# Eight products or seven for Q block 4 and FFN block 12 of the first two chunks, and a head played from words, in a linear attention and FFN kernel

## The chip, the core and the metric

One core of a Trainium2 chip runs the kernel. Its engines are TensorE (PE in the profile; its weight loads are listed as PEld), VectorE (DVE), ScalarE (ACT), GpSimd (POOL) and SyncE (SP, which here only issues DMAs; ACT and POOL can issue them too). Each engine has a queue of its own and takes its instructions in order; semaphores hold an instruction back until what it reads is there. The metric is the time of one execution in microseconds (us), as the median of the runs; the aim is a lower one.

## The reference

`x` has 2048 tokens of D = 640 values. It is normalised over the 640 values, and two branches read the result:

```
xn  = layernorm(x)
q, k, v = xn @ wqkv, cut in three, then into 32 heads of 20
phi(t) = where(t > 0, t + 1, exp(t)) + 1e-6
kv  = sum over tokens of phi(k) (outer) v          # per head
z   = sum over tokens of phi(k)                    # per head
o   = (phi(q) @ kv) / (phi(q) . z + 1e-6)
s   = o @ wo
g   = silu( relu(xn @ w1) @ w2 )                   # w1: 640 x 1728, w2: 1728 x 640
out = x + s * g
```

All tensors are bfloat16.

## The kernel before

**Tiles and stages.** The tokens are 16 tiles of 128, or 4 chunks of 512. Data with the features on the partitions (`xnT`) has 5 blocks of 128 features. FFN columns are 13 blocks of 128 (0 to 12) and a half block of 64; Q columns are 5 blocks (0 to 4). A product block `H j f` (FFN block f of chunk j) or `Q j f` is five matmuls of 128 x 128 by 512 columns, one for each block of features. K is made tile by tile, as five matmuls for each of two halves of 320 columns.

The stages follow each other. The *head* normalises tiles 0 to 7, makes K for them and the first FFN blocks. Then come Q, the rest of K, and the FFN blocks; the product `G` of xn and phi(k) with the denominators; the small products that fold v and wo into one matrix (`kv`, `W`); and last the two output products, `u` for the gate and `o` for the attention, tile pair by tile pair.

**Seven products for eight.** Where two halves of columns meet two halves of the 512 leading features and two chunks, `unit` (line 1169) makes the 2 x 2 block product with seven products and sums of operands (Strassen's scheme in Winograd's form), where eight would be needed. Products 1, 2, 3, 4, 5, 6 and 7 are steps `s1` to `s7`. The fifth block of 128 features is added to products 2, 3 and 4 and, as product 8, to step 7, so that a unit has 2+3+3+3+2+2+2+1 = 18 matmuls. The operand sums are made on VectorE: `h_S`, `q_S`, `m_S` and `k_S` on the weights, `h_T` (`T0` for chunks 0 and 1, `T1` for chunks 2 and 3) on `xnT`. In a unit VectorE also adds pairs of products in PSUM and ScalarE copies two of them. Units are called `a`, `b` (FFN blocks i and i + 6, chunks 0, 1 and chunks 2, 3), `p`, `q` (Q blocks f and f + 2), `k` (K of two tiles), `m` (Q block 4 with FFN block 12), `g`, `u` and `o`. Before the change `m` exists for chunks 2 and 3 alone (`m1`); for chunks 0 and 1 the four blocks are made directly, as `Q04`, `Q14`, `H112`, and FFN block 12 of chunk 0 in the head.

**The head.** K of tiles 0 to 3 and the FFN blocks 4, 5, 10, 11 and 12 of chunk 0 (`HP`) start before the normalisation is known: x is centred (`centre`), transposed on TensorE (`transposes`) and copied out of PSUM (`xcT_copy`), and the factor 1/sigma comes later, for K by the scale of the evacuation, for the FFN blocks by a product with `rsyB` on VectorE (`scale_h`, word `ZS`). Means come from half statistics on VectorE (`bn`) and from an accumulating copy on ScalarE (`mean_act`); variances of all tiles from two `bn_stats` and a `bn_aggr` on VectorE (`bn`, `aggr`; both with the norms in `LN_stats`), and the root from GpSimd. Tiles 4 to 7 are normalised (`LN_norm`) and transposed by a DMA that SP issues (`xnT_dma`, line 702). The order of the head is that of the calls in the source: the loads at the top, then a list of calls for tiles 0 to 3, then five head blocks and four K tiles with the lists `after` of what VectorE is given behind each.

**What sets the order.** Every instruction is recorded with what it reads and writes. From `PROGRAM` (line 343), a list of words, `play` (line 1569) records the work after the head: a word is a step of a unit (`a0.s5`), a block (`H111`), or a piece of work for another engine (`SQ`: the sums `q_S`; `xa`: a load; `n8`: norm of tile 8; `y7`: adding tile 7 of phi(k) to a sum over tokens, by a DMA of GpSimd). `place` (line 189) then puts the records in the order of each engine's queue. TensorE and SP keep the recorded order. The other engines keep it up to `end_of_head`; behind that, the planner takes, by its own costs and due times, one of the next 60 that can run.

**Queues that the change touches.** SP issues, in this order: x tile 0, the K weights in four parts (features 0, 1, 2, and 3 with 4), w1 column groups 2 and 5, x tiles 4 and 5, w1 group 6, x tiles 6 and 7, w1 groups 0 and 3, then the transposes of tiles 4 to 7, x tiles 8 and 9, `wq` (the weights of Q), the transposes of tiles 0 to 3, x tiles 10 and 11, and so on. ScalarE issues x tiles 1, 2 and 3. Column group d of w1 holds FFN blocks 2d and 2d + 1.

Of the kernel before, what the change touches and what calls it, by code (L numbers as in the profile page):

```python
# [4 lines left out]
ALU = mybir.AluOpType  # L5
# [340 lines left out]
H110 H112 H14 H111 T0 H15 SQ SK xa Q14 a0.s1 a0.s5 Q04 a0.s6 p1.s5 p1.s1 n8 wa xb a0.s2 a0.s7 p1.s6 rb a0.s3 a0.s4 p1.s3 a1.s5 a1.s1 wb p1.s7 p1.s2 a1.s6 xc n9 SH1 p1.s4 a1.s2 Kb8 a1.s7 n12 n11 p0.s1 n10 n13 a1.s3 p0.s5 Ka8 p0.s6 n14 a1.s4 n15 y7 p0.s2 a2.s5 a2.s1 p0.s7 Ka12 a2.s6 Kb12 p0.s3 a2.s2 p0.s4 y8 a2.s3 a2.s7 hh0 hh1 T1 a2.s4 b0.s1 b0.s5 Ka11 b0.s6 k1.s1 k1.s5 b0.s2 k1.s6 b0.s7 b0.s3 k1.s7 k1.s2 b0.s4 k1.s3 k1.s4 Kb15 q0.s1 q0.s5 b1.s1 q0.s6 b1.s5 q0.s2 b1.s6 q0.s7 y6 q0.s3 b1.s3 q0.s4 mv6 b1.s7 b1.s2 y2 k2.s5 k2.s1 b1.s4 a3.s5 y3 k2.s6 Kb11 y9 a3.s1 k2.s2 k2.s7 k2.s3 a3.s6 k2.s4 a3.s2 a3.s7 a3.s3 q1.s1 q1.s5 a3.s4 q1.s6 b2.s5 q1.s2 SM y12 b2.s1 y13 Ka15 y0 q1.s7 w2a b2.s6 y4 y1 y14 GT1 GT2 y5 y15 q1.s3 y11 q1.s4 b2.s7 zm b2.s3 GS0 GT3 b2.s2 b3.s1 b2.s4 b3.s5 SH2 y10 b3.s6 m1.s5 m1.s1 b3.s2 b3.s7 m1.s6 b3.s3 m1.s2 b3.s4 m1.s7 zs b4.s5 GT4 m1.s3 b4.s1 m1.s4 c1 b4.s6 b5.s5 b5.s1 w2d c0 b4.s7 b4.s2 b4.s3 b5.s6 b4.s4 g0.s5 w2b g0.s1 b5.s7 b5.s3 b5.s2 zc g0.s6 b5.s4 dn g0.s3 g1.s1 GS1 g1.s5 g1.s6 g0.s7 g0.s2 w2c g1.s7 g1.s3 wv0 ZS uT3 wo do0 g1.s2 g1.s4 g0.s4 wv1 sl rc0 uSa0 uSb0 uT2 uT1 do3 do1 u0.s1 u0.s5 kv1 u0.s6 rc1 kv0 W5 u0.s7 u0.s2 W4 uT4 uSa2 dv1 u0.s3 W2 u0.s4 W1 W3 W0 xre dv0 uSa1 u1.s1 oT uSb2 uSb1 u1.s5 u2.s1 u2.s5 u1.s6 u2.s6 u2.s2 uSa4 u2.s7 oS0 u1.s7 u1.s3 u2.s3 u1.s2 u2.s4 u1.s4 do2 o0.s5 o0.s1 u4.s5 o0.s6 u4.s1 o0.s2 o0.s3 uSb4 o0.s7 u4.s6 o0.s4 u4.s2 o1.s1 oS2 uSa6 u4.s7 oS1 o1.s5 o1.s2 o1.s6 uSa3 u4.s3 o1.s3 o1.s7 u4.s4 o1.s4 u3.s5 o2.s1 u3.s1 rc3 o2.s5 o2.s2 o2.s6 u3.s6 uSb3 o2.s7 dv3 o2.s3 uSa5 u3.s7 o2.s4 u3.s2 o3.s1 rc2 u3.s3 u3.s4 oS3 uSb6 dv2 o3.s2 o3.s5 oS4 o3.s6 u5.s1 u5.s5 o3.s7 o3.s3 uSb5 u5.s6 u5.s2 o3.s4 u5.s7 u5.s3 o4.s1 u5.s4 o4.s5 o4.s2 o4.s6 u6.s1 u6.s5 oS5 u6.s6 o4.s3 o4.s7 u6.s7 o4.s4 u6.s3 oS6 o6.s1 o6.s5 u6.s2 o6.s6 u6.s4 o6.s2 o6.s7 o6.s3 e3 uSa7 o6.s4 u7.s1 o5.s5 o5.s1 u7.s5 o5.s6 u7.s6 o5.s7 o5.s2 o5.s3 u7.s2 o5.s4 e0 f0 uSb7 u7.s7 u7.s3 f3 e1 u7.s4 f1 l0 l1  # L346
# [3 lines left out]
def bass_recurrent_scan__linear_attn_block__dense_activation_relu__prompt_kernel(  # L350
# [292 lines left out]

    def LN_stats(t):
        bn(t, 0)
        bn(t, 1)
        aggr(t)
# [3 lines left out]
    def LN_norm(t):  # L653
        norms.append(sc.op("DVE", lambda eng: eng.tensor_scalar(
            out=xn[:, t, :], in0=xin[:, xs(t), :], scalar1=mv[:, t, 0:1], scalar2=rsy[:, t:t + 1],
            op0=ALU.subtract, op1=ALU.mult), R=[("xin", xs(t)), ("mv", t), ("rsy", t)], W=[("xn", t)]))
        xnT_dma(t)
# [174 lines left out]

    bn(0, 0)
    mean_act(0, HN)
    half_mean_dve(0)
    centre(0)
    mean_act(1, 0)
    transposes(0, 0)  # L840
    xcT_copy(0, 0, 0, "DVE")
    centre(1)
    fill(3)
    K_mm(0, 2, 0, 1)
    transposes(1, 6)
    xcT_copy(0, 0, 1, "DVE")
    mean_act(2, 0)
    xcT_copy(1, 6, 0, "DVE")
    xcT_copy(1, 6, 1, "ACT")
    K_mm(0, 2, 1, KA)  # L850
    K_mm(1, 4, 0, KA)
    centre(2)
# [36 lines left out]
    K_relu(3, 0)
# [397 lines left out]
    def m_unit(jp):  # L1287
        w1l = w1_p[NW - 1]

        def out(half, j, b):  # L1290
            if half:
                sc.op("ACT", lambda eng: eng.activation(out=hT[:, NF - 1, schunk(j)], in_=ps[b], func=ACTF.Relu),
                      R=[("ps", b)], W=[("hT", j, NF - 1)])
# [71 lines left out]
    HP = (4, 5, 10, 11, 12)  # L1365

    def K_tile(t, b):
        K_mm(t, b)
        K_exp(t, b)
        K_relu(t, b)  # L1370
# [157 lines left out]
    def w2_last():  # L1528
# [4 lines left out]
    single = {  # L1533
        "rb": scale_rows,
# [114 lines left out]
    LC = [0, 160, 320]  # L1649
# [252 lines left out]
    def silu_table():  # L1902
# [16 lines left out]
        "oS": o_S,  # L1919
        "st": lambda t: s_tile(t, two_banks()),  # L1920
        "l": s_last,
# [6 lines left out]
        "y": z_add,  # L1928
    }
# [31 lines left out]
```

## Time and profile before

| | us |
|---|---|
| median of the runs | 202.73 |
| lowest, highest of three runs | 202.44, 232.07 |
| span of the profiled execution | 201.4 |
| TensorE busy, share of the span | 197.8, 98% |
| VectorE busy, share of the span | 175.1, 87% |
| ScalarE busy, share of the span | 130.9, 65% |
| GpSimd busy, share of the span | 37.9, 19% |
| DMA: read from HBM, written to it | 15.81 MB, 5.24 MB |

Times come from one profiled execution, with a span of 201.4 us from its first to its last instruction; the runs' median of 202.73 us is 1.3 us more. The granted clock of TensorE is full throughout. "Busy" counts an instruction from its start to its end, and matmuls overlap, so that their pace is read from the distance of their starts, and not from their lengths. Rows of a timeline give start, length, engine, line, operation, output and inputs, count, and in brackets how long the engine had been idle and what ended it. The chain of waits is followed back from the last instruction, at each step to what released it. Names that begin with `reg` are large buffers that hold one thing after another, and buffer numbers are left out; `psT` is PSUM.

### The profile page before, as it was taken

What the parts mean: (1) busy time and instruction counts of PE and PEld (TensorE: products, weight loads), DVE (VectorE), ACT (ScalarE), POOL (GpSimd) and SP (SyncE); (2) the same over time, 40 slices, a digit from 0 to 9 for tenths busy, and PEclk for the clock granted to TensorE, in tenths of its full rate; (3) what the DMA queues carried; (4) which work ended last, traced back from release to release, by engine and by line L of the source; (5) the groups of instructions that cost most, each with busy time, mean ns of one, the idle gap of its engine ahead of it and who ended that gap; (6) DMA issues with size and microseconds to landing.
All of it is one profiled execution on the core that took longest, in us unless ns stands there. A gap on an engine that the chain in (4) does not pass through costs nothing.

```text
span 201.4 us, 3693 instructions
## 1 busy us (share of the span) xinstructions
PE 197.8 (98%) x1340; PEld 122.6 (61%) x1340; DVE 175.1 (87%) x413; ACT 130.9 (65%) x273; POOL 37.9 (19%) x66
## 2 busy tenths in 40 slices
PE   8999999999999999999999999999999999999995
PEld 7655644455455454445654777777777777767773
DVE  5988999999999888999975999999779786985674
ACT  6598957998999999978653224371555555445643
POOL 3174060363134654152200000000000000000000
PEclk9999999999999999999999999999999999999999
DMA  6977974765545896575910987865961244012103
GB/s 196 326 211 120 264 174 30 189 164 119 116 92 107 163 260 131 102 142 104 245 34 2 324 217 207 263 201 145 373 232 65 68 163 165 0 67 68 65 33 98
DMA packets 38471, 30.43 MB, mean 151 GB/s; under 512 B 13749, under 2 KB 38453, under 8 KB 38453
## 3 DMA queue, kind: packets, MB, share of 16 engines
q1 hardware_dynamic: 32581, 23.28, 41.2%
q0 software_dynamic: 4624, 5.57, 14.3%
q10 hardware_dynamic: 1248, 1.35, 2.1%
q8 instruction: 10, 0.16, 0.3%
q14 instruction: 8, 0.07, 0.1%
HBM read 15.81 MB, written 5.24 MB: 105 GB/s over the span
## 4 chain that ended last, share of the span: by engine, by line
PE 95%; DMA 3%; SPq 1%; DVE 0%; issue 0%; DVEq 0%
PE psT L1030 43%; PE psT L1203 31%; PE psT L714 8%; PE psT L804 5%; DMA reg<-in_A_wqkv_dram 3%; PE psT L1501 2%; PE psT L1835 1%; PE psT L822 1%; PE psT L766 1%; PE psT L1626 1%; PE psT L1600 1%; PE psT L934 1%; DVE reg L975 0%; SPq L564 0%; SPq L540 0%
## 5 line engine op out<-in xcount | busy, mean ns | idle before, releaser
L1203 PE MATMUL psT<-reg 128*128 128x512 bf16 (+2 forms) x159 | 41.7, 370 | 0.0
L1030 PE MATMUL psT<-reg,regH 128*128 128x320 bf16 (+1 forms) x224 | 34.8, 299 | 0.0
L1030 PE MATMUL psT<-reg 128*128 128x320 bf16 (+1 forms) x178 | 29.4, 299 | 0.0
L1030 PEld LDWEIGHTS psT<-reg,regH 128*128 128x128 bf16 (+1 forms) x224 | 21.8, 98 | 8.7 <-DVE psT L975 0.2
L1203 PEld LDWEIGHTS psT<-reg 128*128 128x128 bf16 (+1 forms) x159 | 15.5, 98 | 16.1 <-DVE reg L975 0.7
L902 POOL DMA_DIRECT2D regH<-reg x16 | 18.4, 1238 | 27.0 <-DMA regH<-reg 9.4
L1037 ACT ACTIVATE reg<-psT 128x320 f32<-128x320 f32 (+1 forms) x24 | 10.4, 435 | 17.4 <-PE psT L1030 15.9
L1030 PEld LDWEIGHTS psT<-reg 128*128 128x128 f16 (+1 forms) x178 | 17.3, 98 | 7.2 <-DVE regH L1256 0.4
L975 DVE TENSOR_TENSOR reg<-reg 128x1024 f16<-128x1024 bf16 (+10 forms) x30 | 18.9, 645 | 0.7 <-PE psT L1203 0.6
L1253 ACT ACTIVATE regH<-psT 128x512 bf16<-128x512 f32 (+1 forms) x24 | 14.6, 607 | 4.1 <-PE psT L1203 3.9
L975 DVE TENSOR_TENSOR psT<-psT,reg 128x320 f32<-128x320 f32 (+1 forms) x22 | 11.9, 542 | 5.6 <-PE psT L1030 5.1
L1030 PE MATMUL psT<-reg,pqT 128*128 128x320 bf16 (+1 forms) x84 | 16.3, 299 | 0.0
L1662 ACT ACTIVATE wv_sb<-psT 128x320 bf16<-128x320 f32 (+1 forms) x22 | 9.2, 423 | 10.3 <-PE psT L1030 9.9
L635 DVE BATCH_NORM_STATS2 stats<-reg 128x6 f32<-128x320 bf16 x32 | 13.9, 475 | 1.9 <-DMA reg<-in_A_x_dram 1.9
L1850 ACT ACTIVATE reg<-psT 128x640 bf16<-128x640 f32 (+1 forms) x14 | 8.0, 570 | 9.2 <-PE psT L1030 9.2
L714 PE MATMUL psT<-reg 128*128 128x320 bf16 x80 | 12.3, 299 | 0.0
L1037 ACT ACTIVATE psT<-psT 128x320 f32<-128x320 f32 x17 | 7.3, 427 | 6.8 <-PE psT L1030 6.8
L975 DVE TENSOR_TENSOR reg<-psT,reg 128x320 f32<-128x320 f32 (+2 forms) x19 | 9.5, 504 | 1.4 <-PE psT L1030 1.3
L781 ACT ACTIVATE regE<-psT 128x512 bf16<-128x512 f32 x16 | 9.6, 607 | 1.1 <-PE psT L766 0.5
L714 PEld LDWEIGHTS psT<-reg 128*128 128x128 bf16 x80 | 7.8, 98 | 4.3 <-ACT regH L808 0.3
L643 POOL TENSOR_TENSOR rsy<-rsv,mhalf 128x1 f32<-128x1 f32 x16 | 10.0, 622 | 1.3
L1030 PEld LDWEIGHTS psT<-reg,pqT 128*128 128x128 bf16 (+1 forms) x84 | 8.2, 98 | 3.2
(170 smaller groups left out, 397.9 us busy)
## 6 DMA issues: line engine op xcount, KB each, us to landing
regH<-reg POOLq DMA_DIRECT2D x16, 320.0 KB, 3.7
reg<-in_B_w_dram SPq DMA_DIRECT2D x12, 320.0 KB, 4.6
scr<-rden SPq DMA_DIRECT2D x4, 640.0 KB, 6.7
reg<-in_A_x_dram SPq DMA_DIRECT2D x4, 640.0 KB, 6.3
out_dram<-reg SPq DMA_DIRECT2D x14, 160.0 KB, 1.8
regE<-scr SPq DMA_DIRECT2D x3, 640.0 KB, 5.3
reg<-in_A_x_dram SPq DMA_DIRECT2D x4, 320.0 KB, 3.8
reg<-in_A_wo_dram SPq DMA_DIRECT2D x6, 160.0 KB, 5.0
```

What stands on the lines that cost most here:

```text
L635: sc.op("DVE", lambda eng: eng.bn_stats(stats[:, t, a, :], xv[:, HN * a:HN * (a + 1)]), R=[("xin", xs(t))], W=[("stats", t, a)])
L643: sc.op("POOL", lambda eng: eng.tensor_tensor(out=rsy[:, t:t + 1], in0=rsv[:, t:t + 1], in1=mhalf[:, :], op=ALU.pow), R=[("rsv", t), ("mha ...
L714: fns.append(lambda eng, a=a, k=k, lhs=lhs: eng.matmul(ps[bk[a]][:, 0:HN], lhsT=lhs, rhs=wk[:, k, HN * a:HN * (a + 1)], start=(k == 0), st ...
L781: exps.append(sc.op("ACT", lambda eng: eng.activation(out=e_, in_=src, func=ACTF.Exp), R=[key], W=[("er_e", es)]))
L804: sc.group("PE", [(lambda eng, k=k: eng.matmul(ps[b], lhsT=w1_col(k, P * f, P), rhs=src[:, k, :], start=(k == 0), stop=(k == C - 1))) for ...
L902: dma("POOL", lambda eng: eng.dma_start(zacc[a], src, **kw), R=[key] + after, W=[("zacc", a)], chain=zchain[a])
L975: sc.op("DVE", lambda eng: eng.tensor_tensor(out=out, in0=in0, in1=in1, op=op), R=R, W=W, extra=extra)
L1030: sc.group("PE", [(lambda eng, k=k, lhs=lhs, rhs=rhs: eng.matmul(ps[b][:, 0:HN], lhsT=lhs, rhs=rhs, start=(start and k == 0), stop=(k == n ...
L1037: sc.op("ACT", lambda eng: eng.activation(out=dst, in_=ps[b][:, 0:HN], func=ACTF.Copy), R=[("ps", b)], W=[dkey], extra=extra)
L1203: sc.group("PE", [(lambda eng, k=k, lhs=lhs, rhs=rhs: eng.matmul(ps[b][:, 0:nn], lhsT=lhs if tile is None else rhs, rhs=rhs if tile is Non ...
L1253: sc.op("ACT", lambda eng: eng.activation(out=dst, in_=ps[b], func=ACTF.Relu), R=[("ps", b)], W=[("hT", j, f)], extra=ex)
L1662: sc.op("ACT", lambda eng, lo=lo, hi=hi: eng.activation(out=g[:, lo:hi], in_=src[:, lo - HN * n:hi - HN * n], func=ACTF.Silu), R=[key, ("s ...
```

## The change

The four blocks `Q04`, `Q14`, `H112` and FFN block 12 of chunk 0 in the head go; a unit `m0` makes them, on `xnT`, behind `a0`, `p1` and `Kb8`, so that block 12 of chunk 0 no longer needs the product with `rsyB`. The sums `m_S` (`SM`) are wanted sooner for it. For x tiles 1 and 2, the two half statistics and the aggregate on VectorE are replaced by one ScalarE pass that squares the centred tile and accumulates; the norms of these tiles take the mean that is there already.

The head is written as words of `PROGRAM` too, up to the mark `|`, behind which the planner may choose. The words stand in a new order. On SP: x tiles 0 and 2, K weight parts 0 and 1, x tile 3, K weight parts 2 and 3, x tile 4, w1 group 5, x tiles 5 and 7, w1 group 6, x tile 6, w1 groups 2, 0 and 3, then the transposes of tiles 0, 4 and 5, x tiles 8 and 9, transposes of 6 and 7, `wq`, transposes of 1, 2 and 3; x tile 1 alone is left to ScalarE's queue. Tile 0 is normalised ahead of tile 4, and the sum `SH0_1` (of w1 groups 0 and 3) stands in the head's fixed part, behind the norm of tile 6. Behind the head, four blocks (of `HP`), K tiles 4 to 7 and three blocks (`H15`, `H111`, `H110`) come before `a0`. The later words are in another order as well. Of the last tile's two column groups the first is 192 wide and the second 128, where both were 160.

```diff
 PROGRAM = """
-H110 H112 H14 H111 T0 H15 SQ SK xa Q14 a0.s1 a0.s5 Q04 a0.s6 p1.s5 p1.s1 n8 wa xb a0.s2 ...
+lx0 ba0 mh0 lx2 ax1 ma0 ce0 lk01 lk12 ma1 lx3 ma2 lk23 lk35 lx4 lw5 ce1 lx5 lx7 lw6 sq1 lx6 lw2 tr0
+cd0 pf3 cd1 ce2 tr1 lw0 k001 cd2 k012 tr2 bb0 ca3 k101 k112 cd4 k202 k023 k123 ba3 ag0 cd5 ma3 lw3 mh3
+sq2 ce3 k223 S4 N0 S5 N4 k034 tr3 k234 S6 ca7 ca6 N5 k045 k245 ke0 kr0 k135 ke1 lx8 S7 ke2 N6
+SH0_1 bb3 kr1 kr2 ag3 N7 lq N1 N2 |
+S8 k304 k345 N3 ke3 xb F0 kr3 P11 F2 n8 SH0_3 P10 P5 SK rb P4 KT4 F3 xa F1 n12 SH0_2 SH0_4
+wb xc KT5 wa KT6 SH1 KT7 n11 n10 n14 n9 n15 n13 H15 y3 T1 SQ y0 F6 SM F7 T0 F4 H111
+H110 a0.s1 p1.s1 a0.s5 F5 p1.s5 a0.s2 a0.s6 H14 y2 y7 p1.s6 a0.s7 a0.s3 Kb8 y1 p1.s3 a0.s4 p1.s7 Ka8 m0.s1 m0.s5 y8 p1.s4
+p1.s2 m0.s6 Kb12 a1.s1 m0.s2 m0.s7 a1.s5 a1.s6 m0.s3 m0.s4 ...
...
+    BY_ACT = (1, 2)
+
+    def square(t):
+        junk = ek[:, eks(t), 1, :]
+        sc.op("ACT", lambda eng: eng.activation(out=junk, in_=xn[:, t, :], func=ACTF.Square, scale=D ** -0.5,
+                                                accum_out=mv[:, t, 1:2]),
+              R=[("xn", t)] + ([("xn", t, 0)] if t == 0 else []), W=[("mv", t), ("ek_r", eks(t))])
+        sc.allow_unread.add(("ek_r", eks(t)))
+        root(t)
...
     def LN_norm(t):
+        mean, key = (msum[:, t, 1:2], ("msum", t, 1)) if t in BY_ACT else (mv[:, t, 0:1], ("mv", t))
         norms.append(sc.op("DVE", lambda eng: eng.tensor_scalar(
-            out=xn[:, t, :], in0=xin[:, xs(t), :], scalar1=mv[:, t, 0:1], scalar2=rsy[:, t:t + 1],
+            out=xn[:, t, :], in0=xin[:, xs(t), :], scalar1=mean, scalar2=rsy[:, t:t + 1],
...
         def out(half, j, b):
             if half:
-                sc.op("ACT", lambda eng: eng.activation(out=hT[:, NF - 1, schunk(j)], in_=ps[b], func=ACTF.Relu),
+                sc.op("ACT", lambda eng: eng.activation(out=(hT if j else hTh)[:, NF - 1, schunk(j)], in_=ps[b],
...
-    HP = (4, 5, 10, 11, 12)
+    HP = (4, 5, 10, 11)
...
-    LC = [0, 160, 320]
+    LC = [0, 192, 320]
```

In the new words `lx`, `lk`, `lw` and `lq` are loads of x tiles, K weight parts, w1 groups and `wq`; `ax1` is the load by ScalarE; `ba` and `bb` are the first and second half statistics; `ma`, `mh` and `ce` make means and centre; `sq` squares; `tr`, `cd` and `ca` transpose on TensorE and copy out on VectorE or ScalarE; `kTAB` is features A to B-1 of K tile T (`k202`: features 0 and 1 of tile 2); `ke` and `kr` evacuate K; `S`, `N`, `F` are statistics, norm and `K_fin` of a tile; `P` and `KT` are head blocks and K tiles. `root(t)` is the two GpSimd instructions that `aggr` already had.

More of the change, by code (lines that the diff above doesn't have):

```diff
@@ L1928, in bass_recurrent_scan__linear_attn_block__dense_activation_relu__prompt_kernel @@
         "y": z_add,
+        "lx": x_load,
+        "ax": lambda t: x_load(t, 1, "ACT"),
+        "lw": lambda d: w1_load(d, d + 1, "SP"),
+        "ba": lambda t: bn(t, 0),
+        "bb": lambda t: bn(t, 1),
+        "mh": half_mean_dve,
+        "sq": square,
+        "ce": centre,
+        "tr": head_turn,
+        "cd": lambda n: head_copy(n, "DVE"),
+        "ca": lambda n: head_copy(n, "ACT"),
+        "pf": fill,
+        "ag": aggr,
+        "ke": head_exp,
+        "kr": head_relu,
+        "P": head_block,
+        "KT": K_tile,
+        "S": S, "N": N, "F": F,
     }
```

164 lines of the change are left out of this document (72 added, 92 removed).

## The prediction

> **What bounds the kernel now.** I read the shares of the engines first, then the chain of waits, then busy time by stretch.
>
> ```profile
> PE 197.8 (98%) x1340; PEld 122.6 (61%) x1340; DVE 175.1 (87%) x413; ACT 130.9 (65%) x273; POOL 37.9 (19%) x66
> ```
>
> ```profile
> 2.19 5.20 DMA reg<-in_A_wqkv_dram
> 7.38 0.05 issue
> 7.43 1.53 PE psT L714 x10
> ...
> 12.23 5.40 PE psT L804 x25
> 17.62 5.47 PE psT L714 x40
> 23.09 5.40 PE psT L804 x25
> 28.49 1.08 PE psT L766 x5
> 29.57 0.86 PE psT L1203 x4
> ...
> 198.33 0.36 PE psT L1835 x5
> ```
>
> The chain (start, length, what) is TensorE without a break from 7.43, when the third part of the K weights has landed, to 198.69. Products of 512 columns follow each other at 5.40/25 = 0.216 us, those of 320 at 5.47/40 = 0.137. The 2.7 us from there to 201.4 are the last sums and the store. So time falls only if products go or if the unbroken run starts earlier, and every new wait of TensorE adds to it.
>
> ```profile
> core 0: us, PE busy (x) PEld busy (x) DVE busy (x) ACT busy (x) POOL busy (x), PEclk, DMA share, GB/s
> 5.00:10.00 5.00, 4.71 (x46) 3.27 (x44) 4.53 (x17) 2.62 (x8) 0.80 (x2) 1.00 1.08 324
> 25.00:60.00 35.00, 35.00 (x205) 16.85 (x203) 34.71 (x91) 30.61 (x62) 12.78 (x26) 1.00 0.61 125
> ```
>
> The reader is to see the busy time of VectorE (DVE): 34.71 of the 35 us from 25 to 60. It keeps just ahead of TensorE there, and has no room left.
>
> ```profile
> 28.89 0.68 DVE L975 TENSOR_TENSOR regE<-reg 128x1024 f16<-128x1024 bf16 x1
> 29.84 0.59 PE L1203 MATMUL psT<-regE,pqT 128*128 128x512 f16 x2
> ```
>
> The first sum of chunks 0 and 1 (of `T0`; I call it hT1) is done at 29.57; product 5 of unit `a0`, which reads it, starts at 29.84. This margin of 0.27 us is the point to follow.
>
> **Products removed.** `Q04`, `Q14`, the head's block 12 (in `HP`) and `H112` are 4 x 5 = 20 products of 512 columns; unit `m0` has 2+3+3+3+2+2+2+1 = 18. That takes 2 x 0.216 = 0.43 us off the path.
>
> **Head of TensorE.** All 20 transposes and 40 K products stay. The four products of `k202` (0.55 us) now stand ahead of the wait for the third weight part; TensorE is idle for 5.00 - 4.71 = 0.29 us in that stretch, so 0.29 is the most to be had. On SP's queue x tiles 2 and 3, taken from ScalarE's queue, now go out ahead of that part, two issues of some 0.5 us (an SP row below has two in 1.04), but the seven tiles that have to land up to it are the same. If it lands 0.9 later, the 0.55 and the 0.29 nearly make it up, and TensorE loses 0.1. I take -0.29, and +0.1 as the other end.
>
> **Squares on ScalarE.**
>
> ```profile
> 3.79 0.72 ACT L666 ACTIVATE regE<-reg 128x640 bf16<-128x640 bf16 x1
> 4.41 0.19 ACT L666 ACTIVATION_READ_ACCUMULATOR regE<-reg 128x1 f32 x1
> 9.82 5.80 ACT L724 ACTIVATE regE<-psT,rsy 128x640 bf16<-128x640 f32 x8
> ```
>
> The nearest rows are the mean over 640 columns: 0.91 each, 1.8 for two. ScalarE's 5.00 - 2.62 = 2.38 idle us from 5 to 10 hide it. Without that cover the evacuations of K tiles 0 to 3 start later; the fifth, which frees the bank of head block 5, ends at 9.82 + 5 x 0.725 = 13.4, and TensorE gets there at 14.1, so 1.8 of delay would cost 1.1. I take 0. The built program has no further table load.
>
> **VectorE up to hT1.**
>
> ```profile
> 20.24 0.44 DVE L654 TENSOR_SCALAR reg<-reg,mv,rsy 128x640 bf16<-128x640 bf16 x1
> 20.60 0.32 DVE L740 TENSOR_SCALAR regE<-regE 128x640 bf16<-128x640 bf16 x1
> 20.95 0.49 DVE L742 TENSOR_TENSOR reg<-regE 128x640 bf16<-128x640 bf16 x1
> 21.36 0.80 DVE L654 TENSOR_SCALAR reg<-reg,mv,rsy 128x640 bf16<-128x640 bf16 x2
> ...
> 23.72 0.42 DVE L975 TENSOR_TENSOR pqT<-reg 128x512 f16<-128x512 bf16 x1
> 24.06 0.88 DVE L635 BATCH_NORM_STATS2 stats<-reg 128x6 f32<-128x320 bf16 x2
> 24.98 0.21 DVE L639 BATCH_NORM_AGGREGATE mv<-stats 128x2 f32<-128x12 f32 x1
> 25.10 0.37 DVE L975 TENSOR_TENSOR reg<-reg 128x512 f16<-128x512 bf16 x1
> ```
>
> From start to start: a norm 0.36, a `K_fin` 0.76, a sum of 512 columns 0.34 (the one at 23.72 is `SH0_1`), a tile's statistics 1.04, of which 0.46 for each half and 0.12 for the aggregate.
>
> TensorE now comes to product 5 of `a0` sooner. From 12.23 - 0.29 = 11.94 it has four head blocks (4.32), K tiles 4 to 7 (5.47), three blocks (3.24) and four products (0.86): 25.8 on the chain's clock, where it was 29.57 + 2 x 0.216 = 30.0. The work behind that point was 198.69 - 30.0 = 168.7 and grows by 16 products (18 fewer are done ahead of it, 2 are gone), 3.46 us, to 172.15. 25.8 + 172.15 = 197.97, 0.72 less than 198.69, as the two gains say, if nothing waits.
>
> For that hT1 has to come 4.2 us earlier. In the changed order VectorE has, after the norm of tile 6: `SH0_1`; half of tile 3's statistics (0.58); norms 7, 1, 2, 3, 8 (1.80); six `K_fin` (4.56); the statistics of tile 8 and a half of 9 (1.50); six more sums of `h_S` and `q_S` (2.04); then hT1. That is 0.34 + 10.48 + 0.68 = 11.5 us from the start of `SH0_1`. And `SH0_1`, which the head's words put there, reads column groups 0 and 3 of w1, the last two loads of the head:
>
> ```profile
> 9.07 1.04 SPq L560 DMA_DIRECT2D reg<-in_B_w_dram  x2
> reg<-in_B_w_dram SPq DMA_DIRECT2D x1, 320.0 KB, 5.0
> reg<-in_B_w_dram SPq DMA_DIRECT2D x1, 320.0 KB, 7.1
> 16.38 0.39 DVE L654 TENSOR_SCALAR reg<-reg,mv,rsy 128x640 bf16<-128x640 bf16 x1
> ```
>
> Issued at 9.07 and 9.55, they land at 14.1 and 16.6 (issue to landing is the last figure). The bytes ahead of them are the same in both kernels. Before, nobody needs them until 23.72. Now VectorE gets there early: it was through with tile 6's norm at 16.7; less four half statistics and two aggregates of tiles 1 and 2 (2.08) and tile 3's half (0.58), plus norm 0 (0.36), that is 14.4. It waits 2.2 us for a landing at 16.6, or 0.7 if group 3 comes 1.0 behind group 0, as 320 KB at that stretch's 324 GB/s ask. hT1 is then ready at 28.1 or 26.6; TensorE, some 0.2 behind it, ends at 200.45 or 198.95, +1.76 or +0.26. I take the middle, +1.0: the row says 16.6, but its bytes alone don't explain so late a landing.
>
> What else stands behind that wait are norms 7, 1, 2, 3 with their transposes on SP, and the wq load between them.
>
> ```profile
> 20.34 0.47 SPq L545 DMA_DIRECT2D reg<-in_A_wqkv_dram  x1
> 20.86 5.90 SPq L703 DMA_TRANSPOSE reg<-reg  x4
> ```
>
> ```profile
> 14.10 1.50 SPq L703 DMA_TRANSPOSE reg<-reg  x1
> reg<-reg SPq DMA_TRANSPOSE x1, 3.3
> ```
>
> The second pair is tile 4's transpose: issued at 14.1, landed 3.3 later, 1.8 behind the end of its issue. After a late w1, norm 7 ends at 17.9 and its transpose lands by 21.2; K tile 7 wants it at 20.35, so 0.85, inside the wait that follows. The wq load then goes out at 19.4 and three transposes take 3/4 of 5.90: issued by 24.3, landed by 26.1, ahead of hT1.
>
> **The rest.**
>
> ```profile
> 31.98 0.70 DVE L975 TENSOR_TENSOR psT<-psT,wv_sb 128x512 f32<-128x512 f32 x1
> ```
>
> `m0` adds two such sums out of PSUM and a relu (about 0.3) on VectorE, less one row scaling of 0.34, and on ScalarE two copies against one relu saved. They come behind hT1, in a stretch where VectorE has 0.29 us to spare: 0 to +0.7, as far as TensorE isn't late already; I take 0. The other words (units, `W`, divisions) keep every product, and the last cut moves 32 columns from the second group to the first: 0, give or take 0.2.
>
> Sum: the profiled execution ended at 201.4, 1.3 under the median of 202.73. 202.73 + 1.0 = **203.7**.
>
> **Rivals.**
>
> *No wait shows.* If w1 lands by 14.4, hT1 is ready at 25.9 and TensorE waits 0.3: 202.3; with VectorE's idle 0.47 us of 5 to 10 made up too, none: 202.73 - 0.72 = 202.0. For it: before, TensorE was never held although margins were as small. Against it: the landing at 16.6. "Perfetto Trace Analysis", section Identifying the Most-Contended Engine, in the Trainium skill judges VectorE by its busy share and TensorE by its weight loads; by that VectorE (87% against 61%) would be the bound. As a mechanism of this kernel that makes VectorE's net work the gain, 2.08 + 0.34 - 1.70 = 0.7, again 202.0; the unbroken chain on TensorE speaks against it.
>
> *The transposes hold TensorE instead.* Tile 4's transpose landed at 17.4, 0.8 behind w1. Now tile 0's is queued ahead of it, and K tile 4 wants it at 16.26. With 0.5 for 160 KB more at 324 GB/s it lands at 17.9: TensorE waits 1.7 and ends 1.0 late, 203.7, the same time by another wait. "DMA: Bandwidth & Descriptors", section Queues, rings and completion order, in the Trainium skill says that each DMA engine takes descriptors in ring order, so a late w1 always brings this wait along; the 0.8 agrees.
>
> *Slower.* From 32 to 42 us a loop runs over SP: norm of tile 12, its transpose, a w1 load, x tiles 14 and 15, and back to VectorE's statistics of 14, which now stand in its queue ahead of the units' sums.
>
> ```profile
> 34.31 1.53 SPq L560 DMA_DIRECT2D reg<-in_B_w_dram  x1
> DMA to landing us min/median/max: 2.5/4.3/6.8
> ```
>
> VectorE has about 6.5 us of work in between; the loop takes 0.36 for the norm, 5.90/4 = 1.48 and 1.53 for two issues, and the landing of an x load (second row). At the median that is 7.7, a wait of 1.2; at the maximum 10.2, a wait of 3.7, and with the late w1 ahead of it 202.73 + 1.76 + 3.7 = 208.2. It passes 2% where the landing takes over 5.4.
>
> **Numbers.** Forecast, by a late w1 at `SH0_1` or at K tile 4: 0.62. No wait: 0.30. The loop at its worst: 0.07. Over 2% faster, 4.05 us, has no source here: 0.01 (2% is about what a measurement of this kernel can tell from no change). Range: from 202.0 - 0.2 = 201.8 to 202.73 + 1.76 + 1.2 = 205.7.
>
> **What would show it.** Right: VectorE's 512-column sum waits for a w1 load near 15, and TensorE is idle ahead of K tile 4 or of product 5 of `a0`. Wrong: an unbroken chain that ends near 198.0, or a first break behind 30. The 0.43 shows in the count of 512-column products, the 0.29 in the idle time before the first long run.

## The result and the profile after

The changed kernel takes 205.57 us (median; 205.53 to 205.94) against 202.58 us before on the same chip: ratio 1.0149, 95% interval [1.0133, 1.0164], 3.0 us slower. One of the four executions of the kernel before took 232.07 us, and the ratio is that of the others. The profiled execution took 205.58 us with a span of 204.3 us, at the full granted clock.

The engine shares of the page, and the chain of waits (start, length, what) where it leaves TensorE and at its end:

```profile
PE 197.2 (97%) x1328; PEld 122.3 (60%) x1338; DVE 172.3 (84%) x409; ACT 130.1 (64%) x278; POOL 37.4 (18%) x66
```

```profile
12.27 3.20 PE psT L821 x14
15.47 0.02 issue
15.49 0.61 ACT regH L825
16.10 0.22 issue
16.31 0.42 DVE pqT L934
...
22.52 5.86 DMA reg<-reg
...
28.46 0.69 DVE regE L934
...
201.23 0.43 PE psT L1836 x5
```

Before, the chain was TensorE alone from 7.43. Now it runs over a head block, the sum `SH0_1` at 16.31, norms, and a transpose of 5.86 us to the first sum hT1 at 28.46. TensorE ends at 201.66, 2.97 us later than its 198.69 before, which is all of the loss. The timeline of TensorE and its weight loads:

```profile
17.66 5.85 PE L731 MATMUL psT<-reg 128*128 128x320 bf16 x40 [1.13 <-DMA reg<-reg]
28.43 1.04 PE L1162 MATMUL psT<-reg 128*128 128x512 bf16 x4 [1.67 <-DMA reg<-reg]
29.30 1.03 PE L1162 MATMUL psT<-regE,pqT 128*128 128x512 f16 x4
20.61 2.57 PEld L731 LDWEIGHTS psT<-reg 128*128 128x128 bf16 x20 [0.40 <-ACT regE L741]
```

Product 5 of `a0` starts at 29.30 (29.84 before). Without a wait it would have started at 25.64: this is the prediction's 25.8, which is told by the chain's clock, 0.16 later than these rows. So 3.66 us are lost ahead of it. The brackets give 1.67 ahead of `a0`'s first product, 1.13 ahead of K tile 4 and 0.40 at K tile 6. Another 0.29 is the gain at the start that did not come: the weight loads of the head blocks begin at 11.92, and before at 11.93. (The 12.27 of the chain is the second product of the first block. The first has no record; TensorE has 1328 records for 1338 weight loads.) The remaining 0.2 comes from the brackets, which count from the modelled end of a matmul. Nothing of weight is lost behind product 5: 201.66 - 29.30 = 172.36, and the prediction had 172.15 us of work there.

I call the start of product 5 the *gate* of this stage. The rows behind it are those of VectorE (norm 6, `SH0_1`, hT1) and, on SP, the last w1 load, the wq load and the last transpose, each load with its time from issue to landing:

```profile
14.51 0.40 DVE L671 TENSOR_SCALAR reg<-reg,mv,rsy 128x640 bf16<-128x640 bf16 x1
16.31 0.42 DVE L934 TENSOR_TENSOR pqT<-reg 128x512 f16<-128x512 bf16 x1 [1.41 <-ACT regH L825]
28.46 0.69 DVE L934 TENSOR_TENSOR regE<-reg 128x1024 f16<-128x1024 bf16 x1 [1.48 <-DMA reg<-reg]
reg<-in_B_w_dram SPq DMA_DIRECT2D x1, 320.0 KB, 6.9
19.27 0.58 SPq L565 DMA_DIRECT2D reg<-in_A_wqkv_dram  x1
reg<-in_A_wqkv_dram SPq DMA_DIRECT2D x1, 800.0 KB, 6.2
22.52 2.58 SPq L720 DMA_TRANSPOSE reg<-reg  x1
reg<-reg SPq DMA_TRANSPOSE x1, 5.9
```

Before, the first of the four transposes behind wq (issued at 20.86; first line) and the last:

```profile
reg<-reg SPq DMA_TRANSPOSE x1, 5.4
25.48 1.27 SPq L703 DMA_TRANSPOSE reg<-reg  x1
reg<-reg SPq DMA_TRANSPOSE x1, 2.7
```

VectorE is idle twice, for `SH0_1` and for hT1. The first wait is one for the w1 load: issued at 9.35, it landed at 16.2, while the ScalarE instruction that the row names had ended at 16.1. The reader is to see the landing of transpose 3: issued 3 us sooner than before, it lands at 28.4, where it landed at 28.2 before.

### The profile page after: what moved, and what is told of

Its sections match the earlier page's. It is cut to its first block, busy times and chain, and to the rows that moved or that the text cites. A ratio compares the mean times of both kernels' runs of the same rounds, so it can differ in the third digit from the quotient of the medians.

```text
span 204.3 us, 3686 instructions
## 1 busy us (share of the span) xinstructions
PE 197.2 (97%) x1328; PEld 122.3 (60%) x1338; DVE 172.3 (84%) x409; ACT 130.1 (64%) x278; POOL 37.4 (18%) x66
## 4 chain that ended last, share of the span: by engine, by line
PE 75%; DVE 14%; DMA 5%; ACT 2%; issue 2%; SPq 1%; DVEq 0%
PE psT L989 42%; PE psT L1162 21%; PE psT L731 4%; DMA reg<-reg 3%; DVE stats L635 2%; PE psT L1492 2%; DMA reg<-in_A_wqkv_dram 2%; DVE reg L671 2%; DVE psT L934 2%; PE psT L821 2%; DVE reg L934 2%; DVE regH L934 1%; DVE reg L759 1%; PE psT L1836 1%; DVE pqT L934 1%
## 5 line engine op out<-in xcount | busy, mean ns | idle before, releaser
L989 PE MATMUL psT<-reg,regH 128*128 128x320 bf16 (+1 forms) x224 | 35.3, 299 | 0.0
L989 PE MATMUL psT<-reg 128*128 128x320 bf16 (+1 forms) x178 | 28.7, 299 | 0.0
L861 POOL DMA_DIRECT2D regH<-reg x16 | 18.5, 1185 | 25.7 <-DMA reg<-reg 6.8
L934 DVE TENSOR_TENSOR reg<-reg 128x1024 f16<-128x1024 bf16 (+11 forms) x30 | 19.1, 646 | 2.9 <-PE psT L989 2.2
L1663 ACT ACTIVATE wv_sb<-psT 128x320 bf16<-128x320 f32 (+2 forms) x23 | 9.7, 425 | 13.5 <-PE psT L989 13.5
L1212 ACT ACTIVATE regH<-psT 128x512 bf16<-128x512 f32 (+1 forms) x24 | 14.4, 614 | 4.3 <-PE psT L1162 4.0
L934 DVE TENSOR_TENSOR psT<-psT,reg 128x320 f32<-128x320 f32 (+1 forms) x21 | 11.3, 543 | 5.0 <-PE psT L989 4.6
L989 PE MATMUL psT<-reg,pqT 128*128 128x320 bf16 (+1 forms) x84 | 15.5, 299 | 0.0
L635 DVE BATCH_NORM_STATS2 stats<-reg 128x6 f32<-128x320 bf16 x28 | 12.9, 482 | 2.1 <-DMA reg<-in_A_x_dram 2.1
L1169 ACT ACTIVATE psT<-psT 128x512 f32<-128x512 f32 (+1 forms) x18 | 10.6, 596 | 2.4 <-PE psT L1162 2.4
L934 DVE TENSOR_TENSOR psT<-psT,wv_sb 128x512 f32<-128x512 f32 (+1 forms) x14 | 9.1, 653 | 2.0 <-PE psT L1162 1.4
L1851 ACT ACTIVATE reg<-psT 128x640 bf16<-128x640 f32 (+1 forms) x14 | 7.3, 567 | 4.8 <-PE psT L989 4.8
```

The lines of the kernel that those rows point to most:

```text
L635: sc.op("DVE", lambda eng: eng.bn_stats(stats[:, t, a, :], xv[:, HN * a:HN * (a + 1)]), R=[("xin", xs(t))], W=[("stats", t, a)])
L861: dma("POOL", lambda eng: eng.dma_start(zacc[a], src, **kw), R=[key] + after, W=[("zacc", a)], chain=zchain[a])
L934: sc.op("DVE", lambda eng: eng.tensor_tensor(out=out, in0=in0, in1=in1, op=op), R=R, W=W, extra=extra)
L989: sc.group("PE", [(lambda eng, k=k, lhs=lhs, rhs=rhs: eng.matmul(ps[b][:, 0:HN], lhsT=lhs, rhs=rhs, start=(start and k == 0), stop=(k == n ...
L1169: sc.op("ACT", lambda eng: eng.activation(out=dst[:, 0:nn], in_=ps[b][:, 0:nn], func=ACTF.Copy), R=[("ps", b)], W=[dkey], extra=extra)
L1212: sc.op("ACT", lambda eng: eng.activation(out=dst, in_=ps[b], func=ACTF.Relu), R=[("ps", b)], W=[("hT", j, f)], extra=ex)
```

## The experiments

All are edits of the changed kernel, unless the kernel before is named. Medians stand beside those of the kernel before on the same chip. Each run took longer than the range that its theory gave. The *ring* below is what SP has issued and what has not landed yet; *cover* is work of TensorE that stands ahead of the gate.

**The three waits, one by one.** The sum that waited for w1, put behind the head:

```
-SH0_1 bb3 kr1 kr2 ag3 N7 lq N1 N2 |
+bb3 kr1 kr2 ag3 N7 lq N1 N2 |
-S8 k304 k345 N3 ke3 xb F0 kr3 P11 F2 n8 SH0_3 P10 P5 SK rb P4 KT4 F3 xa F1 n12 SH0_2 SH0_4
+S8 k304 k345 N3 ke3 xb F0 kr3 P11 F2 n8 SH0_3 P10 P5 SK rb P4 SH0_1 KT4 F3 xa F1 n12 SH0_2 SH0_4
```

> The first weight sum of h (SH0_1, VectorE 512 columns) taken out of the fixed part of the head and put behind it; all else as in the changed kernel. Theory (the wait of VectorE for the last w1 load is the root): norm 7 starts by 15.5 us for 17.3, tile 7's transpose and the wq load are issued 1.8 us earlier, transposes 1 to 3 land by 26.7 for 28.4, a0's first product no longer waits 1.67 and K tile 6 no longer 0.4; K tile 4's 1.13 stays: 203.6 us (203.3 to 204.2). Rival A (the wq load ahead of transposes 1 to 3 sets them, whatever VectorE does): transposes still land at 28, 205.2 or more. Rival C (the new unit or the new order behind the head costs it): 205.3 or more.

Measured: 205.93 us (before 203.03), ratio 1.0146 [1.0111, 1.0181]: no gain. Timelines of TensorE and of SP:

```profile
27.12 1.04 PE L1162 MATMUL psT<-reg 128*128 128x512 bf16 x4 [0.58 <-DMA reg<-reg]
56.20 0.45 PE L1162 MATMUL psT<-regH,reg 128*128 128x320 f16 x2 [0.67 <-DVE reg L934]
19.34 0.58 SPq L565 DMA_DIRECT2D reg<-in_A_wqkv_dram  x1
```

The wait for w1 is gone, norm 7 starts at 15.93 for 17.30, and yet the wq load goes out at 19.34 (19.27 in the changed kernel): SP issues its transposes one behind the other, and that queue, not VectorE's wait, sets it. `a0` still came 1.3 us sooner in this execution, and gave most of that back at 56 and around it. The 1.3 us can't be put down to the sum either, because the landing of transpose 3 varies by as much: with the sum and SP's order as in the changed kernel it landed at 27.5 in the run with H14 ahead (below), for 28.4; with the sum behind, it landed at 27.1 here and at 28.1 in the run with half statistics. The last section has what goes with that. So the wait that the forecast rested on is real, and taking it away gains nothing at the end.

The wq load behind the transposes (`lq` taken from behind `N7` and put behind `N3`):

> The wq load put behind norm 3, so behind transposes 1 to 3 on SP's queue; all else as in the changed kernel. Theory (late VectorE makes both late; wq's first sums are wanted by the second product behind a0's first): transposes land by 25.5, a0's first product does not wait, but wq lands at 28 or later and the Q unit's first product waits in its place: 205.0 to 206.5. Rival A (wq's place ahead of the transposes is the cause by itself): the 1.67 us ahead of a0's first product goes and nothing takes its place: 203.9.

Measured: 208.70 us, ratio 1.027 [1.0219, 1.0321]. TensorE:

```profile
30.01 0.59 PE L1162 MATMUL psT<-reg 128*128 128x512 bf16 x2 [2.12 <-DMA reg<-in_A_wqkv_dram]
```

Transpose 3 lands at 25.7 now, and wq, issued at 24.17, at 29.9. Either can be early, not both. 1.6 us of the time have a reason that is told in the last section.

The first sum behind the head and tile 4's transpose ahead of tile 0's:

> The first weight sum behind the head, and norm 0 with tile 0's transpose put behind norm 7, so that tile 4's transpose is the first. Theory (the waits add up): beside the first edit's gain the 1.13 us ahead of K tile 4 goes, as its transpose lands by 16.5: 202.5 us (202.2 to 203.3, the upper end where tile 0's transpose now makes transposes 1 to 3 later). Rival B (the order of transposes 0 and 4 alone holds the end and the sum's wait is hidden): no more than 1.1 below the changed kernel, 204.5.

Measured: 206.09 us, ratio 1.0155 [1.0115, 1.0195]. Tile 4's transpose on SP, the first of all, and its landing:

```profile
12.25 1.32 SPq L720 DMA_TRANSPOSE reg<-reg  x1
reg<-reg SPq DMA_TRANSPOSE x1, 5.5
```

It lands at 17.7, no sooner than behind tile 0's (17.5). The loads ahead of it in the ring set it (the last of w1 landed at 17.0), and K tile 4 waits 1.16 us for it (1.13 in the changed kernel). With that wait or less of it (0.47 in the run with the first sum behind) the end is the same.

**The parts of the change.** Variances of tiles 1 and 2 on VectorE again (`BY_ACT = ()`, `sq1` and `sq2` replaced by `ba1 bb1 ag1` and `ba2 bb2 ag2`):

> The changed kernel with the variances of tiles 1 and 2 from VectorE's batch statistics again, at the place where ScalarE's squares stood; two squares of 0.9 us fewer on ScalarE, four statistics and two aggregations (2.2 us) more on VectorE between 5 and 9 us. Theory (the squares are no part of the loss; VectorE's chain of the head moves back by what its idle time of about 1.1 us there doesn't take, and 1.4 us of idle time ahead of the first weight sum takes that): 205.6 us (205.2 to 206.2). Rival D (the squares cost): 204.5 or less.

Measured: 206.34 us (before 202.52), ratio 1.0182 [1.0155, 1.0209]. Without the squares the kernel is no faster, so they are no part of the loss.

The unit undone in the new head, the first time with the fifth head block in the bank that K tile 4 wants (TensorE waited 2.54 us for its evacuation):

> The changed kernel with its unit m0 undone: block 12 of chunk 0 back as the fifth block of the head, block 12 of chunk 1 and Q block 4 of chunks 0 and 1 as products ahead of a0 and after its third step, the six VectorE sums of m0 back to their late place; new head, squares and order kept. 20 products for 18, so 0.43 us more of TensorE work. Theory (the ten products that stood ahead of a0 were the cover of loads and transposes; with them back K tile 4 is wanted at 17.6 and a0's first product near 29, both behind what they wait for): TensorE unbroken again, 202.8 us (202.4 to 203.4), below the changed kernel although it does more. Rival (the new head and order cost it, not the missing cover): 205.5 or more.

Measured: 210.72 us (before 202.52), ratio 1.04 [1.037, 1.043]. Then with other banks:

> The unit undone once more, as in the run before with that edit, where the fifth head block took the PSUM bank that K tile 4 wanted and TensorE waited 2.54 us for its evacuation: here K tiles 4 to 7 take banks 2, 4, 0, 6 (6, 2, 0, 4 there), as free as in the kernel before. That run had further waits of 2.3 us for VectorE and ScalarE between 38 and 50 us, where the order made for the unit now carries two Q blocks and a block. Theory (with the cover back no wait ahead of a0; the waits at 38 to 50 stay): 206.5 us (205.0 to 208.5). Rival (the head itself costs it): TensorE still waits over 1.5 us ahead of a0.

Measured: 211.33 us (before 202.36), ratio 1.044 [1.0393, 1.0487]. This tells little: the first block of chunk 1 now waited 2.58 us for a bank that K tile 7 had filled, and 3.4 us of waits for VectorE and ScalarE at 38 to 50 stayed. Undoing the unit in an order made for it is not the kernel before.

**Can the lost time be had back?** The m sums on GpSimd (`sc.op("POOL", ...)` in `m_S`):

> The run with the first weight sum behind the head, and beside that the four weight sums of the m units (1.1 us of VectorE, 128x256) moved to GpSimd. In that run TensorE came to a0's second product 1.3 us earlier than in the changed kernel and lost 0.67 of it again to a VectorE sum at 56.2 us, with VectorE busy for 29.8 of the 30 us from 30 to 60. Theory (VectorE is the second bound up to 57 us): the wait at 56 goes and the gain of the head is kept, 204.9 us (204.5 to 205.3). Rival (the wait at 56 is one sum's place in the order, not VectorE's load): 205.7 or more.

Measured: 206.26 us (before 202.52). The wait at 56 is gone, and the time isn't better. Norms and transposes 1, 0, 2 as early as they can be:

> The changed kernel with norms and transposes of tiles 1, 0 and 2 put as early as their statistics allow, into the time in which SP's ring still drains the loads; the last w1 load behind the transpose of tile 5, the first weight sum and the load of x tiles 8, 9 behind the head, statistics of tile 3 ahead of norm 7. Theory (SP's queue and the loads ahead of the transposes set the start of a0, VectorE's idle time there sets what follows): transpose 4 lands by 16.5 and K tile 4 waits less than 0.3, wq lands near 24 and transpose 3 by 25, a0's second product starts by 26.6 for 29.3: 202.6 us (202.0 to 203.6). Rival (VectorE bounds it up to 57 us whatever the start): 204.5 or more.

Measured: 208.16 us. Transposes 1, 0, 2 out of the way, wq goes out at 20.93 and transpose 3 still lands at 27.3; `a0`'s first product comes at 27.45 without a wait. My edit had put x tiles 8 and 9 last, and a K tile of theirs waited:

```profile
35.75 0.44 PE L731 MATMUL psT<-reg 128*128 128x320 bf16 x2 [2.34 <-DMA reg<-reg]
```

VectorE relieved by leaving out half the statistics of tiles 9 to 15 (their norms are then not those of the reference), then H14 ahead of `a0`, then both:

```
-        bn(t, 1)
+        if t < 9:
+            bn(t, 1)
```

```
-H110 a0.s1 p1.s1 a0.s5 F5 p1.s5 a0.s2 a0.s6 H14 y2 ...
+H14 H110 a0.s1 p1.s1 a0.s5 F5 p1.s5 a0.s2 a0.s6 y2 ...
```

> The run with the first weight sum behind the head, and the batch statistics of x tiles 9 to 15 taken over the first 320 columns alone: the second half of these statistics is left out, seven VectorE instructions of 0.48 us (some 0.40 each of the engine's time, 2.8 us), most of them between 25 and 57 us. Theory (VectorE, busy for 29.8 of the 30 us from 30 to 60, is the second bound and took the head's gain back at 56): the wait there is gone and the 1.3 us gained ahead of a0 stay: 204.5 us (204.2 to 205.0). Rival (something else takes the gain back): 205.6 or more.

> The changed kernel with block 4 of chunk 1 (H14, five products of 0.216 us) put ahead of a0's first product instead of behind its fourth: 1.08 us of cover given back. TensorE comes to a0's first product at 27.84 instead of 26.76 and still waits some 0.5 for transpose 3 (28.38). Theory (missing cover ahead, VectorE close behind as second bound with a margin of about 0.4): 205.1 us (204.6 to 205.4). If VectorE were no bound: 204.5. Rival (the idle time ahead of a0 isn't what costs): 205.6 or more.

> The run with half statistics for tiles 9 to 15 (left out: the second half of them) and with H14 ahead of a0 beside it. Theory (two bounds, the cover ahead of a0 and VectorE behind it, and both relieved): TensorE comes to a0's first product at 27.6, no wait there, second product at 28.5 with 1.08 us less work behind it: 203.5 us (203.2 to 204.0). Rival (no second bound): the same as H14 and the first sum would give without the left-out statistics; that run isn't made, so this one counts against 204.5, the best of either alone.

Measured: 206.13, 206.69 and 206.86 us (before 202.36). With half the statistics VectorE is busy for 29.16 of the 30 us from 30 to 60 (29.83 in the run with the first sum behind), and nothing is gained. In this execution product 5 of `a0` started at 29.00, so the 1.3 us that were to be kept were not there to keep; but TensorE, 0.3 sooner at product 5 than in the changed kernel, was 0.7 later at the end. VectorE's load by itself is not the second bound that I took it for. With H14 ahead, TensorE and VectorE at 32 us:

```profile
31.60 0.24 DVE L934 TENSOR_TENSOR regH<-reg 128x256 f16<-128x256 bf16 x1
31.76 0.49 DVE L635 BATCH_NORM_STATS2 stats<-reg 128x6 f32<-128x320 bf16 x1
32.16 0.69 DVE L934 TENSOR_TENSOR psT<-psT,wv_sb 128x512 f32<-128x512 f32 x1
32.90 0.60 PE L1162 MATMUL psT<-regX,reg 128*128 128x512 f16 x2 [1.44 <-DVE psT L934]
```

The wait ahead of `a0` is gone and another stands 4 us on, at the sums of products that follow transpose 3. VectorE did statistics and m sums first, which suggested the planner: it counts with landings up to 3.9 us earlier than the profile shows. With those made later in `place`:

```
+                c.end += next((g for t, g in self.LATER if c.end < t), 0.0)
+    LATER = ((14.0, 0.0), (23.1, 2.0), (24.5, 3.9), (27.0, 3.0), (29.0, 2.0), (32.0, 0.8))
```

> The changed kernel, its planner counting with landings as the profile of the changed kernel shows them (for transfers that it lets land from 14 to 32 us 0.8 to 3.9 us later than its own estimate); the words, the head, TensorE's and SP's order are the same, only ScalarE's, VectorE's and GpSimd's order behind the head can change. Theory (the order was made for landings that the chip doesn't keep, but behind 29.3 us TensorE has no wait left to lose): 205.4 us (204.8 to 205.9); a0's first product still at 28.4. Rival (the planner's order costs by itself even here): 204.5 or less.

> H14 ahead of a0, with the planner's landings corrected in the same way; against the run with H14 ahead alone (206.69). Theory (the 1.44 us at 32.9 there are VectorE's order, made for earlier landings): that wait is gone or under 0.4, 1.08 us of TensorE work stand in the gap ahead of a0: 204.6 us (204.2 to 205.3). Rival (transpose 3 and the sums behind it set the products at 33 us, whatever the order): 205.7 or more, with a wait of over 1 us between 30 and 34.

> As the run before, with the first weight sum behind the head beside it. Theory: transpose 3 lands by 27.5, a0's second product starts by 28.3 with 1.08 us less behind it, no wait of over 0.5 at 56: 204.0 us (203.5 to 204.8). Rival (a second bound other than the planner's order): 205.4 or more.

Measured: 206.47, 206.85 and 206.35 us (before 202.47), all at ratios of 1.019 to 1.020. In the third, VectorE and TensorE:

```profile
28.77 0.28 DVE L936 TENSOR_TENSOR regH<-regH,reg 128x256 f16<-128x256 f16 x1
29.37 0.44 DVE L673 TENSOR_SCALAR reg<-reg,mv,rsy 128x640 bf16<-128x640 bf16 x1
30.13 0.69 DVE L936 TENSOR_TENSOR regE<-reg 128x1024 f16<-128x1024 bf16 x1
30.88 1.04 PE L1164 MATMUL psT<-regE,pqT 128*128 128x512 f16 x4 [1.52 <-DVE regE L936]
```

Transpose 3 landed at 28.2, but VectorE was given m sums and a norm up to 30.13 and came to hT1 two microseconds late. The planner's landings are wrong for the changed head, but correcting them moves the wait and doesn't remove it.

**The missing cover.** The kernel before, its work, loads and head unchanged, with three groups of five products moved behind `a0`. The first time the blocks of chunk 1 fell on a bank just filled (TensorE waited 1.62; 207.05 us); then:

```
-H110 H112 H14 H111 T0 H15 SQ SK xa Q14 a0.s1 a0.s5 Q04 a0.s6 p1.s5
+H110 H14 H111 T0 H15 SQ SK xa a0.s1 a0.s5 a0.s6 H112 p1.s5
...
-p1.s3 a1.s5
+p1.s3 Q14 a1.s5
...
-p1.s4 a1.s2
+p1.s4 Q04 a1.s2
...
-    last_use = [0] * 8
+    last_use = [-4, -3, -2, 0, 0, 0, -1, 0]
```

> The kernel before with block 12 of chunk 1 and Q block 4 of chunks 0 and 1 moved behind a0's first products as in the earlier run (205 to 207 there), the blocks of chunk 1 now in PSUM banks 0, 1, 2, 6. Theory (the products ahead of a0 covered transposes 1 to 3 and the sums behind them): no wait of over 0.5 us between 23 and 27 us, TensorE wants a0's first product at 27.2 and waits for transpose 3 at 28.2, further waits for VectorE's sums up to 45 us; with the same work as the kernel before 205.0 us (204.0 to 206.2). Rival (the earlier loss was the bank's): 202.4 to 203.3.

Measured: 206.96 us (before 202.62), ratio 1.0216 [1.019, 1.0241]: 4.3 us for the order of 15 products, where 205.0 was expected. TensorE:

```profile
28.33 0.61 PE L1203 MATMUL psT<-reg 128*128 128x512 bf16 x2 [0.78 <-DMA reg<-reg]
29.89 0.60 PE L1203 MATMUL psT<-regE,pqT 128*128 128x512 f16 x2 [0.95 <-DVE regE L975]
32.87 0.60 PE L1203 MATMUL psT<-regE,pqT 128*128 128x512 f16 x2 [0.69 <-ACT regH L808]
42.11 0.61 PE L1203 MATMUL psT<-regE,reg 128*128 128x512 f16 x2 [0.87 <-DVE wv_sb L975]
```

Product 5 of `a0` starts at 29.89, where it started at 29.84 with the 10 products in front. So 10 products, 2.16 us, went behind a gate that stayed where it was, and are paid in full. The other half of the loss is another thing: behind product 5 TensorE is idle for 2.0 us, the last two rows and smaller waits, where the kernel before has none.

And the unit alone in the kernel before (`HP` without 12; `H112`, `Q14`, `Q04` out; `SM` and `m0.s1` to `m0.s4` in, behind `p1.s7`), without that bank wait:

> The kernel before with the unit m0 alone, as in the earlier run (207.84 there), the blocks of chunk 1 in PSUM banks 0, 1, 2, 6. Theory (the unit takes 15 products away ahead of a0's products 5 and 6 and puts 13 behind; transpose 3 lands at 28.2 whatever it does): no wait for ScalarE between 22 and 26, in its place one for transpose 3 or its sums at 27 to 31; 206.4 us (205.0 to 207.5), as slow as the changed kernel or slower although its head is the old one. Rival (the earlier loss was the bank's): 202.0 to 203.3.

Measured: 208.70 us (the profiled execution 207.87), ratio 1.0299 [1.0245, 1.0353]; with the bank wait 207.84 (expected 202.3). Two of the four executions without it, 209.5 and 209.8 us, had a lower clock (last section). TensorE:

```profile
28.23 0.61 PE L1203 MATMUL psT<-reg 128*128 128x512 bf16 x2 [1.13 <-DMA reg<-reg]
29.85 0.61 PE L1203 MATMUL psT<-regE,pqT 128*128 128x512 f16 x2 [1.01 <-DVE regE L975]
39.85 1.25 PE L1203 MATMUL psT<-reg 128*128 128x512 bf16 x5 [0.70 <-ACT pqT L783]
```

Again the gate stays, at 29.85, with 13 products, 2.8 us, more behind it; TensorE is idle for another 1.5 us behind it. The old head with the unit is slower than the changed kernel. No version tried is faster than the kernel before.

The gate in one table, from the profiled executions (us). The two rows with "sum behind" have the first sum behind the head too:

| kernel | transpose 3 lands | `a0` product 5 starts | execution |
|---|---|---|---|
| before | 28.2 | 29.84 | 202.73 (median) |
| changed | 28.4 | 29.30 | 205.58 |
| first sum behind | 27.1 | 28.00 | 205.43 |
| m sums on GpSimd, sum behind | 27.7 | 28.70 | 206.27 |
| half statistics, sum behind | 28.1 | 29.00 | 206.28 |
| early norms | 27.3 | 28.31 | 208.10 |
| H14 ahead | 27.5 | 28.93 | 206.33 |
| before, cover moved | 28.3 | 29.89 | 207.09 |
| before, unit alone | 28.2 | 29.85 | 207.87 |

## Why the prediction was wrong

The kind was right: TensorE's unbroken chain, waits ahead of `a0`, slower by less than 2%. The size was not, +3.0 for +1.0, and the cause is another one than it put first. That 205.57 lies just within the range is luck: its upper end, 205.7, takes 1.2 us from the loop at 32 to 42 us, which did not appear.

*Products removed, work behind `a0`.* Right. The weight loads went from 1340 to 1338, and 172.15 us stood as 172.36.

*Head of TensorE.* Nothing was gained, where -0.29 was forecast, with +0.1 as the other end. The wait did not go; TensorE has one of 0.30 us at 6.32, now for the second part of the K weights.

*Squares.* Right: with them undone, the kernel is not faster.

*VectorE up to hT1.* Right as worked out. VectorE was through with norm 6 at 14.9 (14.4 forecast) and waited 1.41 us for w1 (landed at 16.2), between the 0.7 and 2.2 given. hT1 was ready at 29.15; without its own wait of 1.48 for transpose 3 that is 27.7, in the 26.6 to 28.1 forecast.

*What stands behind that wait.* Here the prediction failed: "issued by 24.3, landed by 26.1, ahead of hT1". The issue ended at 25.1, and the landing came at 28.4. The wq load went out at 19.27 (19.4 forecast) but landed at 25.5, and the three transposes follow it in the ring, at 27.1, 27.8 and 28.4. I had priced them by tile 4's transpose, 1.8 us behind the end of its issue, which had no more than the rest of a w1 load ahead of it (landed at 16.6), and let them pass a load of 800 KB. The trace before had the better row: there the first transpose behind wq took 5.4 us and landed at 26.3, 0.7 behind wq. The prediction itself cited the Trainium skill, "DMA: Bandwidth & Descriptors", section Queues, rings and completion order, that each DMA engine takes descriptors in ring order; these landings agree with it, and I used it for w1 alone.

*The sum.* The term that was too small is hT1: 27.35 in the middle of the forecast, 29.15 measured, 1.8 of the 2.0 us by which the forecast fell short. What set it was not VectorE's wait for w1, which taken away gained nothing, but the landing of transpose 3. No order brought that below 27.1 except the one with wq behind it. What the loss consists of is the work that TensorE no longer has until then. The change takes 18 products, 3.9 us, from ahead of `a0`'s product 5, and puts 16, 3.46 us, behind it; with the gate at 29.30 for 29.84 that is -0.54 + 3.46 = +2.9, the measured loss. The kernel before, with its products moved and nothing removed, loses 2.2 us in the same way; the rest of its 4.3 are waits behind the gate, which the changed kernel does not have.

*Rivals.* The transposes did hold K tile 4 (1.13 us; 1.7 forecast), beside the other wait and not in its place; it is swallowed by the gate behind it. Tile 0's transpose was not the reason. No wait shows: no. VectorE's net work as the gain: no; its busy time fell from 175.1 to 172.3 us, and the kernel became slower. (The section of the Trainium skill that the prediction names there, Identifying the Most-Contended Engine in "Perfetto Trace Analysis", asks for MFU, the matmuls' share of peak, beside TensorE's weight loads; the prediction left MFU out.) The loop at 32 to 42 us did not appear: TensorE has no wait there.

*Open.* An earlier gate has not been turned into time. In the table the gate of the kernels with the new head lies between 28.0 and 29.3, and the executions take 205.4 to 208.1 us, the changed kernel with the latest gate among the shortest. With the first sum behind, the 1.3 us go in waits for VectorE and ScalarE of under 0.7 us, most of them at 55 to 57 us, the rest by 64. Neither VectorE's load nor the planner's landings by themselves explain them; what sets that stretch was not settled.

## What to carry to other kernels

Work that leaves the front of a kernel is worth its length only if the bound engine has other work until the next stage's last input lands: find that landing, and price what is moved behind it in full. Price a transfer by what its ring still holds, not by its own length: the same transpose took 2.7 us and 5.9 us to land. A wait that the profile names may be hidden by a later gate, and taking it away then gives nothing.

## What the runs showed of the hardware

**Behind a gap of TensorE of 2 us the clock can be halved.** Stretches of the run with wq behind (the granted clock is the last figure but two), whose TensorE had been idle for 2.12 us at 30.0:

```profile
core 0: us, PE busy (x) PEld busy (x) DVE busy (x) ACT busy (x) POOL busy (x), PEclk, DMA share, GB/s
28.00:32.00 4.00, 1.99 (x8) 0.91 (x9) 3.58 (x11) 1.94 (x5) 1.45 (x2) 0.91 1.14 288
32.00:34.00 2.00, 2.00 (x6) 0.73 (x5) 0.72 (x2) 0.81 (x2) 0.00 (x0) 0.50 0.15 49
34.00:36.00 2.00, 2.00 (x9) 0.74 (x8) 1.59 (x6) 0.60 (x1) 0.84 (x2) 0.82 0.00 0
```

The three rows miss 0.36, 1.00 and 0.36 us of full clock, so some 3.4 us passed at half of it. Three of the four executions show a lower mean clock, 0.992, and took 208.7 to 208.9 us; the fourth kept the full clock and took 207.09, so it cost 1.6 us. The first run with the unit undone, with a gap of 2.54 us, shows the same in three of its four executions, but there without a difference in time (210.6 to 210.8 us with it, 210.7 without). Gaps of 2.34 us, in the run with early norms, and of 2.58 us, in the second run with the unit undone, left the clock of the profiled execution alone, so the length of the gap is not all that decides. In the run with the unit alone two executions had the lower clock, and the profiled one, which did not, has no gap over 1.2 us; what lowered it there is not known.

**An instruction fetch shares the DMA engines.** While the last w1 load is under way, the queues' list from 13.6 to 14.9 us of the changed kernel has

```profile
q8 instruction: 1, 0.02, 5.8%
```

one packet of 16 KB that takes 1.2 us of one of the 16 DMA engines (5.8% of 16 in 1.3 us). The load, w1 group 3, lands 1.9 us behind group 0, which has the same size. That the fetch makes it late was not tried, but the other traces go with it. Where such a packet starts by 13.0 us (3 runs), group 3 lands 0.9 to 1.1 us behind group 0; where it starts from 13.2 to 14.15 (15 runs, both kernels among them), 1.3 to 2.5; where it starts at 14.24 (1 run), 0.9 again.

The landing of transpose 3 has a like companion, a packet of 8 KB on another instruction queue (us):

| kernel | wq lands | packet starts | transposes 1, 2, 3 land |
|---|---|---|---|
| changed | 25.5 | 25.5 | 27.1, 27.8, 28.4 |
| H14 ahead | 24.6 | 25.1 | 25.3, 26.9, 27.5 |
| m sums on GpSimd, sum behind | 24.9 | 24.4 | 26.4, 27.2, 27.7 |
| first sum behind | 25.2 | 23.9 | 25.8, 26.5, 27.1 |

In the 19 traces with wq ahead of the transposes, one of these lands 1.4 to 1.7 us behind the transfer ahead of it in ten, and in those ten the packet starts within 0.7 us of the landing of wq. In the other nine it starts 1.3 us or more ahead of that, and the steps are 0.5 to 0.9 us. So some 1.0 us of the changed kernel's gate goes with a fetch, and so does most of the 1.3 us by which the run with the first sum behind was sooner. It is not shown which of the two causes the other, or whether a third thing causes both.
